# The first four expert weights issued ahead of GpSimd's wait for the queries of pair 4, and later landings entered in PE's plan

## Chip, cores and metric

One core of a Trainium2 chip. The metric is the device time of one execution in microseconds; the kernel before was run 13 times, and its time is the median of these. Engines are named as in the profile: PE (TensorE, matmul; PEld its weight loads), ACT (ScalarE), DVE (VectorE), POOL (GpSimd), SP (SyncE, here only issuing transfers).

## The reference

Two stages. The first is attention with 8 batches, 12 heads, 448 tokens and a head size of 64, with soft-capped scores and no mask. The second takes its output as 448 tokens of width 768 and runs four attention experts of head size 64 with a causal mask; a gate picks two of the four for each token and weighs them.

```python
scores = scale * np.matmul(q, k.transpose(0, 1, 3, 2))
scores = cap * np.tanh(scores / cap)
scores = scores - np.max(scores, axis=-1, keepdims=True)
attn = np.exp(scores)
attn = attn / (np.sum(attn, axis=-1, keepdims=True) + 1e-09)
attn_out = np.matmul(attn, v)
x = attn_out.transpose(0, 2, 1, 3).reshape(B, S, H * D)

logits = x @ w_gate
topk = np.argpartition(-logits, K, axis=-1)[..., :K]
...
for e in range(E):
    q = x @ wq[e]
    k = x @ wk[e]
    v = x @ wv[e]
    scores = scale * (q @ k.transpose(0, 2, 1))
    ...
    ye = a @ v @ wo[e]
    for kk in range(K):
        mask = topk[:, :, kk] == e
        out += mask[..., None] * w[:, :, kk:kk + 1] * ye
```

All inputs are float32. The weights `wq`, `wk` and `wv` are (4, 768, 64), `wo` is (4, 64, 768).

## The kernel before

**Pairs and batches.** The heads are taken two at a time: 48 pairs, 6 to a batch. For a pair, POOL casts queries, keys and values from float32 to float16 (`a_cast`, `a_castv`, lines 385 to 404; DVE does the queries of pairs 0 and 1), PE transposes queries and keys (`a_tr`, L414 to L421), DVE copies them out of PSUM, PE makes the scores in four parts (`fill`, L476 for the part of the tail keys, L480 for the rest), ACT takes tanh of each part (`tanh`, L510) and then one exponential over the pair (`expo`, L516), PE multiplies with the values (L544, L550), DVE divides, and PE transposes the result (L585) into `xT`, the second stage's input. Two score buffers stand between PE and ACT.

**The second stage.** When the six pairs of a batch are in `xT`, its expert work becomes available: `batch(b)` puts it into PE's list. The projections of queries and keys run for two experts at a time, r = 0 for experts 0 and 1 and r = 1 for experts 2 and 3 (`b_qk`, L724); the projection of values takes all four experts and the gate in one matmul of 260 columns (`b_v`, L640, tile `wvg`), so it needs the value weights of all four; scores and exponentials follow (L762, L781), then values, the transposes and the output projection (L863). The work of batch b runs among the pairs of batch b + 1. The last batch is ordered by a separate search at the end (`last_batch`).

**The weights.** They come in through transfers issued by POOL, which convert to float16 on the way (line 1067). The list `loads` holds sixteen, in this order: q and k of expert 0, q and k of expert 1, v of experts 0 to 3, q and k of expert 2, q and k of expert 3, o of experts 0 to 3. Below they are called q0, k0, v0 and so on. The transfers of a pair's queries, keys and values are issued by SP (L308, L312), from pair 4 on for two pairs at a time; they land in float32 buffers that the casts empty.

**What sets the order.** The program is one walk over ACT's order, `prog`: tanh and exponential of pair after pair. A pair's entry `("S", p)` calls `slot(p)`, which issues what goes with it, in this order: SP's loads some pairs ahead, POOL's cast of pair p + 4, two weights on POOL, constants (slots 4 and 5), and it puts the transposes, the value products and, at every sixth pair, the batch's projections into PE's list. Every engine runs its instructions in the order in which they were issued, so the two weights of slot 0 stand behind the cast of pair 4 in POOL's order.

PE's order is made when the program is built. `Plan` keeps a reckoned time for each engine (`plan.act`, `plan.pe`, `plan.dve`) and, in `plan.done`, a reckoned time at which each thing is ready; `step` takes from PE's list what can start earliest and, among what can start within 0.3 of that, what is due first. Matmuls on dummy data (`keep_warm`, L898) fill places where nothing else can start. The reckoned landing of a weight decides only where PE's work on it is put in the order; on the chip, PE waits at that place until the weight has landed. A weight kind with several transfers, such as `("w", "v")`, takes the value entered last.

In the planner's figures a pair takes ACT 2.83 for the four tanh parts and 2.71 for the exponential (`dur`), the walk starts at 7.0, and so slot 1 is called near 9.8, slot 2 near 15.4, and so on by 5.55.

Of the kernel before, what the change touches and what calls it, by code (L numbers as in the profile page):

```python
# [239 lines left out]
def kernel(  # L240
# [13 lines left out]
    nc = tc.nc  # L254
# [39 lines left out]
    def load(p, n=2):  # L294

        b, j = divmod(p, HP)
        h0, h1 = 2 * j, 2 * (j + n)
        qf = stage.tile([QP, 2 * n, QC * Dh], f32, name=f"qf_{p}", tag="qf")
        kf = stage.tile([128, 2 * n, KC * Dh], f32, name=f"kf_{p}", tag="kf")
        vf = stage.tile([128, 2 * n, KC * Dh], f32, name=f"vf_{p}", tag="vf")  # L300
        ktf = stage.tile([128, n, Dh], f32, name=f"ktf_{p}", tag="ktf")
        vtf = stage.tile([128, n, Dh], f32, name=f"vtf_{p}", tag="vtf")
        for i in range(n):
            h = slice(2 * i, 2 * i + 2)
            staged[p + i] = (qf[:, h], kf[:, h], vf[:, h], ktf[:, i], vtf[:, i])

        def rows(dst, src, c):
            return lambda eng: eng.dma_start(dst, src.rearrange("h (p c) d -> p h (c d)", c=c))  # L308

        def tails(dst, src, i):  # L310
            t = src[b, h0:h1, KM:S].rearrange("(j two) p d -> two p j d", two=2)
            return lambda eng: eng.dma_start(dst[64 * i : 64 * (i + 1)], t[i])  # L312

        return [
            rows(qf, q[b, h0:h1], QC), rows(kf, k[b, h0:h1, 0:KM], KC), tails(ktf, k, 0),
            tails(ktf, k, 1), rows(vf, v[b, h0:h1, 0:KM], KC), tails(vtf, v, 0), tails(vtf, v, 1),
        ]
# [6 lines left out]
    def ahead(p, n, since, more=4):  # L324

        new = range(p + n + more * (p > since), p + n + more * (p >= since) + 1)
        return [i for i in new if i < NP]
# [48 lines left out]
    def a_cast(p):  # L376
        if p >= NP:
            return
        eng = nc.vector if p < 2 else nc.gpsimd
        assert p < 8 or ("tr", p - 8) in plan.done  # L380
        assert p < 12 or ("pv", p - 12, 1) in plan.done
        qf, kf, vf, ktf, vtf = staged.pop(p)
        q16 = hd.tile([QP, QC, 2, Dh], f16, name=f"q16_{p}", tag="q16", bufs=8)
        k16 = hd.tile([128, KC, 2, Dh], f16, name=f"k16_{p}", tag="k16", bufs=8)
        eng.tensor_copy(q16, qf.rearrange("p h (c d) -> p c h d", c=QC))  # L385
        nc.gpsimd.tensor_copy(  # L386
            k16, kf.rearrange("p h (c d) -> p c h d", c=KC)
        )
        for g in range(2):
            r = slice(64 * g, 64 * (g + 1))  # L390
            eng.tensor_copy(ktz[p % 8][r, r], ktf[r, :])
        cast[p] = (q16, k16)
        vcast[p] = (vf, vtf)
        if p > 1:
            a_castv(p)
# [506 lines left out]
    plan = Plan()  # L902
# [35 lines left out]
    def b_const(i):  # L938
        if i == 0:
            nc.gpsimd.memset(ltm, 0.0)  # L940
            nc.gpsimd.affine_select(
                out=ltm, in_=ltm, compare_op=ALU.is_ge, fill=-60000.0, base=0,
                pattern=[[1, 128]], channel_multiplier=-1,
            )
        else:
            nc.vector.memset(vtL, 0.0)
            nc.vector.memset(vtL[64:128, :, Dh : Dh + 1], 1.0)
        nc.vector.memset(vtB[i], 0.0)
        nc.vector.memset(vtB[i][0:64, 0:E:2, Dh : Dh + 1], 1.0)
        nc.vector.memset(vtB[i][64:128, 1:E:2, Dh : Dh + 1], 1.0)  # L950
        for t in pB[2 * i : 2 * i + 2]:
            nc.vector.memset(t[:, 0:64], 0.0)
# [8 lines left out]
    loads = []  # L961
# [81 lines left out]
    for p in range(len(UNITS), NP + HP + 4):  # L1043
        nom.setdefault(("S", p), t)

    def slot(p):

        plan.work[:] = [u for u in plan.work if u["key"][0] != "warm"]
        n = 9 if p < 3 else 6 if p < 7 else 3 if p < 13 else 0
        for i in range(n):  # L1050
            plan.done["from", p, i] = nom["S", p] + 7.0 + 5.6 * i / n
            plan.add(("warm", p, i), 0.22, 0.0, [("from", p, i)], 1.0e9, keep_warm)
        if p % 2 == 0:
            for i in ahead(p, LOAD, DEEP):
                if i % 2 == 0:
                    for f in load(i):
                        f(nc.sync)
        for i in ahead(p, CAST, DEEP + 2):
            a_cast(i)
            plan.done[("cast", i)] = max(  # L1060
                5.65 * i + 1.5 if i < 12 else 0.0,
                plan.act + 4.0 + 3.5 * (i - p - CAST) * (p == DEEP + 2),
            )
        for _ in range(2):
            if loads:
                w, dst, src = loads.pop(0)
                nc.gpsimd.dma_start(dst, src)
                plan.done["w", w] = plan.act + 26.0
        if p in (4, 5):
            b_const(p - 4)  # L1070
        for i in (1, 2) if p == 0 else ahead(p, TR, DEEP + 4, 4):
            plan.add(("tr", i), 0.43, 0.95, [("cast", i)], nom["S", i] - 3.0, a_tr, i)
        if 1 <= p < len(UNITS):
            u = UNITS[p - 1]
            es = [("E", u)]
            due = nom["S", p + 1] + 2.0
            if isinstance(u, tuple):
                i = "AB".index(u[1])
                u = u[0]
                plan.parts(("pv", u, i), 2, 0.47, 0.55, es, due, a_pv, u, i)  # L1080
                d = [("pv", u, i)]
                plan.add(("xt", u, "AB"[i]), 0.12, 0.27, d, due, a_xt_part, u, i)
            else:
                plan.parts(("pv", u, 0), 2, 0.47, 0.55, es, due, a_pv, u, 0)
                d = [("pv", u, 0)]
                plan.parts(("pv", u, 1), 2, 0.47, 0.55, d, due, a_pv, u, 1)
                plan.add(("xt", u), 0.22, 0.35, [("pv", u, 1)], due, a_xt, u)
        if p >= HP and p % HP == 0 and p < NP:
            batch(p // HP - 1)
        if p == NP - 1:  # L1090
            last_qk()
        if p == NP:
            last_vg()
# [6 lines left out]
    def last_qk():  # L1100
        for r in range(2):
            g = ("qk", "A", r)
            due = nom["X", B - 1, r, 0] - 2.0
            for j in range(NDC):
                d = [x_of(j, "A"), ("w", ("q", r)), ("w", ("k", r))] + [(*g, j - 1)] * (j > 0)
                plan.add(
                    (*g, j), 0.22, 0.66 * (j == NDC - 1), d, due, qk_mm, "A", r, j,
                    aux={0: "open", NDC - 1: "close"}.get(j), group=g,
                )
# [10 lines left out]
    def batch(b):  # L1120
        x = ("xt", HP * b + HP - 1)
        t0, t1 = nom["X", b, 0, 0], nom["X", b, 1, 0]
        for r, t in enumerate((t0, t1)):
            plan.parts(("q", b, r), 3, 1.13, 0.55, [x, ("w", ("q", r))], t - 4.0, b_qk, b, r, "q")
            plan.parts(("k", b, r), 3, 1.13, 0.55, [x, ("w", ("k", r))], t - 4.0, b_qk, b, r, "k")
        for n in range(4):
            d = [("v", b, n - 1)] if n else [x, ("w", "v")]
            plan.parts(("v", b, n), 2, 0.66, 0.6, d, t0 + 2.0 * n, b_v, b, n)
        plan.add(("g1", b), 0.0, 1.0, [("v", b, 3)], t1 + 1.0, b_gate, b, aux=None)
        plan.add(("g", b), 0.0, 0.8, [("g1", b), ("G", b)], t1 + 3.0, b_gate2, b, aux=None)  # L1130
        for e in range(E):
            due = t1 + 6.0 + 3.0 * e
            d = [("X", b, e // 2, 1), ("g", b)] + [("pvB", b, e - 1)] * (e % 2)
            plan.add(("pvB", b, e), 0.31, 0.7, d, due, b_pv, b, e)
            if e % 2:
                plan.add(("oT", b, e // 2), 0.22, 0.35, [("pvB", b, e)], due, b_ot, b, e // 2)
        for n in range(4):
            for f in range(2):
                i = 2 * n + f
                d = [("oT", b, 1), ("w", "o")] if i == 0 else [("wo", b, *divmod(i - 1, 2))]  # L1140
                due = t1 + 19.0 + 1.5 * i
                plan.add(("wo", b, n, f), 0.33, 0.5, d, due, b_wo, b, n, f)
# [522 lines left out]
```

## Time and profile before

| | |
|---|---|
| median of 13 runs | 326.75 us |
| lowest and highest of the 13 | 322.79 and 331.34 us |
| time of the profiled execution | 328.0 us |
| its span in the profile | 326.2 us |
| PE busy | 285.9 us (88%) |
| DVE busy | 217.8 us (67%) |
| POOL busy | 157.9 us (48%) |
| share of the chain that ended last: ACT, PE, DMA | 67%, 19%, 4% |
| DMA share in the windows 20 to 30, 30 to 40, 40 to 50 and 50 to 60 us | 1.15, 1.40, 1.61, 1.37 |

The span is what the profile covers of the execution; the execution's own time has a little more around it. An engine's order of time gives each instruction's start and length, its line and operation, and in brackets how long the engine had stood idle before it and what it then waited for. A window's row gives the busy time of each engine with its number of instructions, then the clock granted to PE as a share of full speed, the mean busy share of the 16 DMA engines, and GB/s. [...] Queue 1 is that of SP's transfers, queue 0 that of POOL's.

### The profile page before, as it was taken

The page shows a single profiled execution, that of the slowest core. Times are in us where ns is not written, and L with a number is a line of the kernel's source. Part 1 is how long each engine was busy: PE and PEld are TensorE (multiplying, and loading weights), DVE is VectorE, ACT ScalarE, POOL GpSimd, SP SyncE. Part 2 cuts the span into 40 slices and gives each one's busy share as a digit, 9 for nine tenths or more (in the row PEclk, how much of TensorE's full clock was granted, in tenths as well). Part 3 has the DMA queues.
Part 4 walks back from the last instruction along what each step waited for, and adds up shares of the span by engine and source line. Part 5 has one row for each costly group of instructions (what it writes and reads, how often), then busy time and mean ns, then how long its engine had stood idle before and what let it go on. Part 6 is the DMA issues. An engine that isn't in the chain of part 4 may idle for free.

```text
span 326.2 us, 9088 instructions
## 1 busy us (share of the span) xinstructions
PE 285.9 (88%) x3439; PEld 179.7 (55%) x3439; DVE 217.8 (67%) x760; ACT 306.8 (94%) x311; POOL 157.9 (48%) x480
## 2 busy tenths in 40 slices
PE   8888874998999979998889969997899888999993
PEld 3455442655556555655646645655655664557762
DVE  4444440667776787669867886668766976578673
ACT  3999993899999999999999999999999999999973
POOL 3739999482923569982932568062915100220200
PEclk9999996999999999999999999999799999999998
DMA  7689999997012999759073852677011102020045
GB/s 165 172 225 234 215 219 224 218 221 174 2 51 99 254 260 248 208 179 234 4 193 123 222 144 87 183 219 193 3 50 70 53 2 97 2 75 2 3 169 171
DMA packets 65404, 46.22 MB, mean 142 GB/s; under 512 B 26000, under 2 KB 61968, under 8 KB 65360
## 3 DMA queue, kind: packets, MB, share of 16 engines
q1 hardware_dynamic: 54064, 43.28, 50.9%
q0 software_dynamic: 10512, 1.58, 6.9%
q10 hardware_dynamic: 784, 0.77, 0.8%
q8 instruction: 27, 0.44, 0.6%
q14 instruction: 17, 0.14, 0.1%
HBM read 36.19 MB, written 11.01 MB: 145 GB/s over the span
## 4 chain that ended last, share of the span: by engine, by line
ACT 67%; PE 19%; issue 5%; DMA 4%; DVE 2%; POOL 1%; DVEq 0%; POOLq 0%
ACT y L510 32%; ACT p L516 26%; ACT pBs L781 7%; DMA wvg<-in_moe_wv_dram 4%; PE vps L640 2%; PE wops L863 2%; PE pv L550 2%; PE dummy L898 2%; PE pv L544 1%; PE s L480 1%; PE kps L724 1%; PE qkA L1166 1%; PE qps L724 1%; PE s L476 1%; PE qkB L1166 1%
## 5 line engine op out<-in xcount | busy, mean ns | idle before, releaser
L510 ACT ACTIVATE y<-s 128x896 f16<-128x896 f32 (+1 forms) x176 | 138.5, 933 | 6.9 <-PE s L476 6.0
L516 ACT ACTIVATE p<-y 128x3136 f16<-128x3136 f16 x44 | 128.7, 2925 | 0.1
L789 POOL TENSOR_SCALAR_AFFINE_SELECT pBs<-pBs 128x128 f16<-128x128 f16 (+1 forms) x112 | 28.3, 279 | 110.5 <-ACT pBs L781 109.4
L550 PE MATMUL pv<-v16s,p 128*128 128x65 f16 x1056 | 56.3, 194 | 0.0
L480 PE MATMUL s<-qt,kt 64*128 64x448 f16 x264 | 47.5, 363 | 9.4 <-ACT y L510 7.2
L550 PEld LDWEIGHTS <-p 128*128 128x128 f16 x1056 | 47.6, 98 | 3.7 <-issue 0.2
L544 PE MATMUL pv<-vtzs,p 128*128 128x130 f16 x176 | 39.6, 225 | 9.4 <-ACT p L516 7.6
L559 DVE RECIPROCAL rc<-pv 128x4 f32<-128x4 f32 x96 | 17.3, 180 | 43.0 <-PE pv L550 41.9
L563 DVE TENSOR_TENSOR xk<-pv,rc 128x256 f16<-128x256 f32 x96 | 40.8, 425 | 3.3
L370 DVE COPY ob<-wops 128x384 f32<-128x384 f32 (+1 forms) x54 | 29.9, 554 | 6.9 <-PE wops L863 6.6
L640 PE MATMUL vps<-wvg,xT 128*128 128x260 f16 (+1 forms) x192 | 30.6, 277 | 4.2 <-DMA wvg<-in_moe_wv_dram 4.2
L544 PEld LDWEIGHTS <-p 128*128 128x128 f16 x176 | 17.1, 97 | 28.9 <-ACT p L516 15.8
L480 PEld LDWEIGHTS <-kt 64*128 64x128 f16 x264 | 16.0, 93 | 29.8 <-issue 23.0
L385 POOL CAST q<-qf 112x512 f16<-112x512 f32 x46 | 28.2, 613 | 7.2 <-DMA qf<-in_q_dram 5.4
L781 ACT ACTIVATE pBs<-sB 128x960 f16<-128x960 f32 (+1 forms) x28 | 30.7, 1112 | 0.0
L863 PE MATMUL wops<-wo,oT 128*128 128x384 f16 x128 | 30.6, 327 | 0.0
L399 POOL CAST v16s<-vf 128x384 f16<-128x384 f32 x48 | 24.4, 508 | 6.0 <-DMA vf<-in_v_dram 3.2
L386 POOL CAST k<-kf 128x384 f16<-128x384 f32 x48 | 24.4, 508 | 3.4 <-DMA kf<-in_k_dram 3.4
L370 DVE COPY xT<-xtp 128x448 f16<-128x448 f16 (+2 forms) x50 | 18.6, 374 | 8.7 <-PE xtp L585 7.7
L404 POOL CAST vtzs<-vtf 64x64 f16<-64x64 f32 x96 | 22.8, 238 | 2.9
L898 PE MATMUL dummy<-warm 128*128 128x512 f16 x67 | 22.1, 418 | 1.3 <-DVE warm L330 1.3
L640 PEld LDWEIGHTS <-xT 128*128 128x128 f16 x192 | 16.4, 98 | 11.7 <-DMA wvg<-in_moe_wv_dram 4.7
(180 smaller groups left out, 536.4 us busy)
## 6 DMA issues: line engine op xcount, KB each, us to landing
qf<-in_q_dram SPq DMA_DIRECT2D x22, 448.0 KB, 5.7
out_dram<-ob SPq DMA_DIRECT2D x23, 384.0 KB, 2.3
kf<-in_k_dram SPq DMA_DIRECT2D x22, 384.0 KB, 6.3
vf<-in_v_dram SPq DMA_DIRECT2D x22, 384.0 KB, 5.6
out_dram<-ob SPq DMA_DIRECT2D x8, 192.0 KB, 2.8
ktf<-in_k_dram SPq DMA_DIRECT2D x44, 32.0 KB, 5.4
vtf<-in_v_dram SPq DMA_DIRECT2D x44, 32.0 KB, 4.8
kf<-in_k_dram SPq DMA_DIRECT2D x4, 192.0 KB, 3.3
```

Source lines behind the costliest of these rows:

```text
L370: (nc.scalar.copy if act else nc.vector.tensor_copy)(dst, src)
L480: nc.tensor.matmul(sc[:, g, 0:S], kt[r, 128 * i : 128 * (i + 1)], qt[r, :], start=True, stop=True,)
L510: nc.scalar.activation(dst, src, AF.Tanh, scale=isc / capf)
L516: nc.scalar.activation(pt[:, 0:n], y.pop(u)[:, 0:n], AF.Exp, scale=capf)
L544: nc.tensor.matmul(pv[:, n, :, :], prob(p, w, 0, 0), vtz[p % 12], start=(n == 0), stop=False, skip_group_check=True,)
L550: nc.tensor.matmul(pv[:, n, g, :], prob(p, w, j, g), v16[p % 12][:, g, j - 1, :], start=False, stop=(j == KC), skip_group_check=True,)
L563: nc.vector.tensor_tensor(xt[p][:, 2 * i : 2 * i + 2, :, :], pv[:, :, :, 0:Dh], rc.broadcast_to((128, 2, 2, Dh)), ALU.mult,)
L640: nc.tensor.matmul(ps, xT[b][:, j, w : w + 128], wvg[:, j, 0 : ps.shape[1]], start=(j == 0 and first), stop=(j == NDC - 1), skip_group_che ...
L781: nc.scalar.activation(pb[:, o0 : o0 + n], st[b].pop(("sc", r, g))[:, 0:n], AF.Exp, scale=isc)
L789: nc.gpsimd.affine_select(out=blk, in_=blk, compare_op=ALU.is_ge, fill=0.0, base=0, pattern=[[1, n]], channel_multiplier=-1,)
L863: nc.tensor.matmul(ps, st[b]["oT", r][:, w : w + 128], wo2[r][:, f * (D // 2) : (f + 1) * (D // 2)], start=(r == 0), stop=(r == 1),)
L898: nc.tensor.matmul(dummy, warm[:, 0:128], warm, start=True, stop=True)
```

## The change

In slot 0, four weights (q0, k0, q1, k1) are issued before the cast of pair 4, where two were issued after it; they are entered in the plan as landed at 30.0. In every later slot two weights are issued behind the cast, as before, so that each later pair of weights goes one slot earlier: v0 and v1 in slot 1, v2 and v3 in slot 2, q2 and k2 in slot 3, q3 and k3 in slot 4, the output weights in slots 5 and 6. Their reckoned landing was 26 behind ACT's reckoned time; it becomes the later of 20 behind it and 37.0 + 4.2 p for slot p.

```diff
+    def load_weights(n, done):
+        for _ in range(min(n, len(loads))):
+            w, dst, src = loads.pop(0)
+            nc.gpsimd.dma_start(dst, src)
+            plan.done["w", w] = done
+
     def slot(p):
...
+        if p == 0:
+            load_weights(4, 30.0)
         for i in ahead(p, CAST, DEEP + 2):
             a_cast(i)
...
-        for _ in range(2):
-            if loads:
-                w, dst, src = loads.pop(0)
-                nc.gpsimd.dma_start(dst, src)
-                plan.done["w", w] = plan.act + 26.0
+        if p:
+            load_weights(2, max(plan.act + 20.0, 37.0 + 4.2 * p))
         if p in (4, 5):
             b_const(p - 4)
```

## The prediction

> **What bounds the kernel now.** I read the page's busy shares first, then the waits of each engine, then the order of time around the one long wait, then the DMA queues. The shares:
>
> ```profile
> span 326.2 us, 9088 instructions
> ...
> PE 285.9 (88%) x3439; PEld 179.7 (55%) x3439; DVE 217.8 (67%) x760; ACT 306.8 (94%) x311; POOL 157.9 (48%) x480
> ```
>
> ScalarE (ACT) is busy for 306.8 of 326.2 us; PE follows with 285.9, of which 22.1 are dummies (L898). From 7.24 us, its first tanh, to the tail at 310 us it has one stretch of idleness. The order of time on ScalarE (start, length, work, idle before it) shows it:
>
> ```profile
> 44.13 2.87 ACT L516 ACTIVATE p<-y 128x3136 f16<-128x3136 f16 x1
> 46.84 2.59 ACT L510 ACTIVATE y<-s 128x896 f16<-128x896 f32 x3
> 54.44 0.54 ACT L510 ACTIVATE y<-s 128x448 f16<-128x448 f32 x1 [5.02 <-PE s L476]
> 54.88 2.81 ACT L516 ACTIVATE p<-y 128x3136 f16<-128x3136 f16 x1
> 57.59 1.72 ACT L510 ACTIVATE y<-s 128x896 f16<-128x896 f32 x2
> 60.23 0.92 ACT L510 ACTIVATE y<-s 128x896 f16<-128x896 f32 x1 [0.93 <-PE s L480]
> 61.31 0.54 ACT L510 ACTIVATE y<-s 128x448 f16<-128x448 f32 x1 [0.16 <-PE s L476]
> ```
>
> The reader is to see three gaps, 5.02 + 0.93 + 0.16 = 6.11 us; nothing else but 0.34 us at 235.8 idles ScalarE in the middle of the run. Its waits are for scores from PE, so PE's order of time over the same place:
>
> ```profile
> 48.41 0.54 PE L724 MATMUL qps<-xT,wq 128*128 128x448 f16 x2
> 53.20 0.83 PE L640 MATMUL vps<-wvg,xT 128*128 128x260 f16 x3 [4.25 <-DMA wvg<-in_moe_wv_dram]
> 53.82 0.58 PE L476 MATMUL s<-qt,kt 128*128 128x448 f16 x1
> ```
>
> PE had the first batch's queries begun, came to the projection on the value weights (L640) at 48.95 and stood 4.25 us for the last of them. The next scores (L476, pair 8) are behind it in PE's order, so ScalarE ran dry. The windows around it give PE's granted clock, the number before the DMA share:
>
> ```profile
> 48.90:53.20 4.30, 0.05 (x2) 0.01 (x1) 0.36 (x1) 0.52 (x1) 4.07 (x11) 0.72 1.52 238
> 53.20:57.20 4.00, 4.00 (x25) 1.97 (x26) 0.00 (x0) 2.76 (x2) 3.72 (x11) 0.50 1.38 208
> ```
>
> After the wait PE ran at 0.50, with no idle time: the 0.93 and 0.16 us that follow are this backlog. GpSimd's order of time says why the weights are late:
>
> ```profile
> 17.18 0.53 POOL L404 CAST vtzs<-vtf 64x64 f16<-64x64 f32 x2
> 21.55 0.61 POOL L385 CAST q<-qf 112x512 f16<-112x512 f32 x1 [3.84 <-DMA qf<-in_q_dram]
> 25.43 0.84 POOL L1067 DMA_DIRECT2D wq<-in_moe_wq_dram  x1
> 38.08 1.65 POOL L1067 DMA_DIRECT2D wvg<-in_moe_wv_dram  x2
> ```
>
> GpSimd waits 3.84 us for pair 4's queries, and only behind that cast come the weights. The issues looked up one at a time (start of issue plus time to landing) give the landings: q0 25.43 + 5.4 = 30.8; q1 29.66 + 10.2 = 39.9; v0 33.87 + 11.7 = 45.6; v2 38.08 + 12.8 = 50.9; v3 38.90 + 14.25 = 53.15 (the chain of waits gives this last one); q3 47.03 + 14.7 = 61.7; k3 47.88 + 17.9 = 65.8. Latency grows while spacing stays: the queue is backed up and delivers a weight every (53.15 - 30.8) / 7 = 3.2 us. What counts is when the queue starts, not when each weight is issued.
>
> **The change, part by part.** *The first four issues move ahead of the cast of pair 4.* Four at 0.83 us (row L1067) are 3.3 us, from 17.71, where the last cast before the wait ends, to 21.05. The cover is the 3.84 us wait, so they cost nothing on GpSimd, with 0.5 us to spare; without that cover the cast would be 3.3 us late. Queued behind are the casts of pairs 4, 5 and on, and PE's transposes wait for those. As two fewer issues lie between casts 4 and 5, cast 5 starts 1.65 us earlier, at about 25.5, and every later piece of GpSimd's order likewise as far as its data are there. SP's loads, which wait for these casts, aren't held by this.
>
> *The queue starts 7.7 us earlier* (25.43 to 17.75). At the same spacing v3 lands at 53.15 - 7.7 = 45.5. It must be issued in time: order is now four weights, casts 4 and 5, v0, v1, cast 6, v2, v3. Casts 5 and 6 take 2.55 us each, so v0 goes at about 28.0 and v3 at 33.0 if pair 6's data are there, at 34.0 if they are late as priced below; with the longest wvg time to landing, 14.25, that is 48.2. So 45.5 to 48.2, against 48.95 when PE gets there. I take 45.5, since the queue's spacing is the steadier row. **The wait of 4.25 goes whole**, with PE's cold stretch: -6.11 us on ScalarE.
>
> *What the earlier weights collide with.* Pair 4's loads are in flight: queries issued 15.78 (5.7 us), keys 16.38 (6.3 us, landing 22.7), and PE's transposes of pair 4 run at 23.49 to 24.1, right behind the key casts (the last ends at 23.69). The first weight's packets moved 2.5 us behind its issue (13 packets by 28.0, 771 in the next 2 us), so now from 20.2: the keys are exposed for 2.4 us. Rows: a value load issued at 24.06 was exposed for 1.8 us and took 5.7 us, no more than before (5.7 to 6.0); a query load issued at 26.04 was exposed 4.6 us and took 1.0 longer than its like (6.6 for 5.6); the keys at 26.74 1.5 longer. That is 0 to 0.23 us per us, for pair 4's keys 0 to 0.6 us. Slack behind the transposes is 0.67 us of PE idle and 0.15 at the next scores, 0.8 in all. Taken: 0. The worst row is a stretch where SP's queue moved 0.25 MB in 2 us (34 to 36) where it otherwise moved some 0.5: half speed, keys 2.4 late, 1.6 us lost on ScalarE. Nearest rows in time and kind are the first, so I keep 0 and hold 1.6 for the range.
>
> The Trainium skill speaks against this: its page "DMA: Bandwidth & Descriptors", section "Queues, rings and completion order", says that each DMA engine takes turns between the queues that have work, a packet at a time. By that rule two backed-up queues get equal turns, and pair 4's keys would go at half speed, 1.6 us lost and a time of 323.6 in place of 322.0. The row of 24.06 shows no such loss over 1.8 us, while the stretch of 34 to 36 looks like the rule.
>
> *Pair 6 and later.* Issued 21.05 to 24.06 by SP, landing 26.7 to 29.8 before; exposed from 20.2 on, at 0.23 per us they come up to 2.2 us late, 32.0 for the values. PE transposed pair 6 at 35.01, for which the key casts must be done. If loads took the worst measured 10.6 us, the keys of pair 6 (issued 21.65) would land at 32.3 and their two casts, about 1 us, end at 33.3: 1.7 us of cover are left. Pair 8 (transposed at 47.31, cast at 39.77 to 41.3) has more. Cost 0.
>
> *PE's order reckons otherwise.* Before, a weight was entered as landing 26 us behind ScalarE's planned time. With the planner's 5.55 us for a pair, slot 3 stands at 20.9 and the value weights at 46.9, 6 us too early against 53.15. Now slot 2's entry is 37 + 8.4 = 45.4, which is where I put v3. The second pair of experts (q2 to k3) goes from slot 5 (32 + 26 = 58.0; measured 65.8) to slot 4, 37 + 16.8 = 53.8. My landing for k3 is 17.75 + 5.4 + 11 x 3.2 = 58.3, for q3 55.1: the plan is 1.3 to 4.5 us too early there. Before, PE began that q at 66.68 and k at 71.25, which without the 6.1 us is 60.6 and 65.1. If the order stays, nothing waits. If it moves up to 53.8, q waits 1.3, and PE's dummies (at 60.71, 61.11 and 63.78, so three of them in this stretch) hide a part. Bounds 0 and 4.5; I take 0.6, nearer to the end where the order stays, since the value blocks come due first.
>
> *Everything else in the order* is planned by the same greedy walk from slightly other times; rows for its effect there are none. By the one ScalarE gap (0.34 us) between 62 and 310, and its tail gaps of 0.17 to 0.85, I bound it at -0.9 to +0.9 and take 0.
>
> **Sum.** Span 326.2 - 6.1 + 0.6 = 320.7. The profiled execution took 328.0, 1.8 more than its span: 322.5. That execution is 1.25 above the median of 326.75 and within 322.79 to 331.34. If the wait's length is what spreads the runs, the kernel after is at 322.5 whatever the run; if all runs spread alike, it is 321.3. I go between: **322.0**.
>
> **Rivals.** (1) *Part of the wait stays, or the second experts' weights take its place* (PE standing at L724 for k3). For it: the reckoned 53.8 against 58.3; against: the distance to 60.6. Half of what is won given back: 322.0 + 3 = 325.0, range 323.8 to 326.
>
> (2) *It doesn't do what it says*: the weights start earlier but the engines are full (DMA share over 1.0 from 20 to 70 us), so v3 lands at 53 anyway. For it: the weight spacing of 3.2 us is set by sharing; against: the packets are the same and the queue delivered its first weight in 5.4 us in the same full traffic. Time 326.75.
>
> (3) *Slower*: 4 x 768 small packets ahead of pair 4's and 6's loads starve the casts, PE stands at the transposes (L414) and ScalarE behind it. It decides once pair 4's keys come over 0.8 + 6.1 = 6.9 us late, at 29.6. For it: the transposes sit right on the casts. Against: the longest load in the busiest stretch took 10.6 for 6.3, 4.3 more, 3.5 us lost after the slack. With that delay back for pair 6 without its cover, another 4.3, and the planner's wait at k3 of 4.5 on top, 12.3 in all: 322.0 - 0.6 + 12.3 = 333.7; for the mechanism at the break-even of 6.9 it is 328, and I put the case at 331.
>
> **How the numbers follow.** Forecast 0.79, with its own range 320.2 to 323.7 (the 1.6 us above, 0.9 of order either way and half the spread below); rival 1 0.09, rival 2 0.06, rival 3 0.06. The range of 8 in 10 runs from 319.9 to 325.1, over most of rival 1. 0.5% of 326.75 is 1.6 us, about what a measurement of this kernel can tell from no change: faster means below 325.1, slower above 328.4. Faster 0.79 + 0.05 = 0.84; same 0.09 (the rest of rival 1, most of rival 2); slower 0.07.
>
> **What would show it.** In the profile after: first weight issue near 17.8 us; cast of pair 4's queries at 21.5 to 22.2; last wvg landing at 45 to 48; no wait at L640; PE's clock 1.0 from 48 to 57; ScalarE without a gap over 1 us up to 310; 94% busy to 96%. I am wrong if wvg still lands past 49, if ScalarE idles at 25 to 36, or if PE stands at L724 near 54 to 58.

## The result, and the profile after

| | before | after |
|---|---|---|
| median | 325.83 us (48 runs) | 321.29 us (11 runs) |
| lowest to highest | 322.42 to 331.34 us | 320.83 to 324.66 us |
| profiled execution, its span | 328.0 and 326.2 us | 321.09 and 319.3 us |
| ScalarE's gaps between 49 and 62 us in it | 6.11 us | none over 0.15 us |
| last value weight (v3) issued, landed | 38.90, 53.15 us | 34.50, 44.4 us |
| PE's first value matmul (L640) | 53.20, after 4.25 of waiting | 48.48, no wait |

The ratio of after to before is 0.9893, 95% interval 0.9862 to 0.9923: faster by 1.1%. It leaves out executions that took over 1.5% more than the fastest of their kernel; for the kernel before these are its longest, the profiled 328.0 among them, so the gain is smaller than the medians give (4.5 us, 1.4%). The prediction was 322.0 us, in a range of 319.9 to 325.1.

ScalarE's order of time after, at the place of the old gaps (start, length, instruction; an idle time would stand in brackets):

```profile
43.82 2.87 ACT L516 ACTIVATE p<-y 128x3136 f16<-128x3136 f16 x1
46.53 3.21 ACT L510 ACTIVATE y<-s 128x896 f16<-128x896 f32 x4
49.64 2.81 ACT L516 ACTIVATE p<-y 128x3136 f16<-128x3136 f16 x1
52.35 2.99 ACT L510 ACTIVATE y<-s 128x896 f16<-128x896 f32 x4
55.23 2.81 ACT L516 ACTIVATE p<-y 128x3136 f16<-128x3136 f16 x1
```

Four tanh parts and an exponential follow each other without a bracket, and an idle time of over 0.15 us would have one. From the first tanh at 6.92 us to the tail at 303 us there is none. PE's order of time after:

```profile
48.10 0.54 PE L724 MATMUL qps<-xT,wq 128*128 128x448 f16 x2
48.48 0.50 PE L640 MATMUL vps<-wvg,xT 128*128 128x260 f16 x3
48.81 0.35 PE L476 MATMUL s<-qt,kt 128*128 128x448 f16 x1
...
54.59 0.54 PE L724 MATMUL qps<-xT,wq 128*128 128x448 f16 x2
```

The same three pieces as before, in the same order, with no wait between them; the last line is the first use of the second experts' queries, which stood at 66.68 before. The windows after, granted clock before the DMA share:

```profile
48.90:53.20 4.30, 4.30 (x49) 2.42 (x47) 2.00 (x6) 4.21 (x5) 3.95 (x13) 1.00 1.37 220
53.20:57.20 4.00, 4.00 (x50) 2.51 (x46) 2.43 (x10) 4.00 (x5) 3.25 (x10) 1.00 1.19 192
```

The clock that fell to 0.72 and 0.50 stays at 1.00. GpSimd's order of time after:

```profile
17.83 0.84 POOL L1049 DMA_DIRECT2D wq<-in_moe_wq_dram  x1
...
20.28 0.85 POOL L1049 DMA_DIRECT2D wk<-in_moe_wk_dram  x1
21.17 0.61 POOL L385 CAST q<-qf 112x512 f16<-112x512 f32 x1
22.22 0.51 POOL L386 CAST k<-kf 128x384 f16<-128x384 f32 x1 [0.43 <-DMA kf<-in_k_dram]
22.67 0.53 POOL L391 CAST ktzs<-ktf 64x64 f16<-64x64 f32 x2
24.78 0.51 POOL L399 CAST v16s<-vf 128x384 f16<-128x384 f32 x1 [1.59 <-DMA vf<-in_v_dram]
...
33.67 1.65 POOL L1049 DMA_DIRECT2D wvg<-in_moe_wv_dram  x2
```

The four issues fill the old wait, and the query cast starts as they end. The values of pair 4 now come late (1.59 us), which nobody on the path waits for: ScalarE has no gap behind it.

### The profile page after: what moved, and what is told of

Same layout as the page of the kernel before. It is cut to its first block, busy times and chain, and to the rows that moved or that the text cites. A ratio compares the mean times of both kernels' runs of the same rounds, so it can differ in the third digit from the quotient of the medians.

```text
span 319.3 us, 9087 instructions
## 1 busy us (share of the span) xinstructions
PE 283.6 (89%) x3438; PEld 178.7 (56%) x3438; DVE 217.9 (68%) x760; ACT 306.5 (96%) x311; POOL 158.1 (50%) x480
## 4 chain that ended last, share of the span: by engine, by line
ACT 74%; PE 16%; issue 5%; DVE 1%; DMA 1%; POOL 1%; DVEq 0%; POOLq 0%
ACT y L510 35%; ACT p L516 30%; ACT pBs L781 7%; PE vps L640 2%; PE wops L863 2%; PE pv L550 2%; DMA qf<-in_q_dram 1%; PE s L480 1%; PE pv L544 1%; PE qkA L1171 1%; PE pvB L808 1%; PE qkB L1171 1%; PE sB L762 1%; PE kps L724 1%; PE xtp L608 1%
## 5 line engine op out<-in xcount | busy, mean ns | idle before, releaser
L640 PE MATMUL vps<-wvg,xT 128*128 128x260 f16 (+1 forms) x192 | 30.3, 275 | 0.0
L391 POOL CAST ktzs<-ktf 64x64 f16<-64x64 f32 x92 | 21.6, 234 | 2.7
L898 PE MATMUL dummy<-warm 128*128 128x512 f16 x66 | 21.0, 408 | 1.3 <-DVE warm L330 1.3
```

Of the source, the lines that this page charges most:

```text
L640: nc.tensor.matmul(ps, xT[b][:, j, w : w + 128], wvg[:, j, 0 : ps.shape[1]], start=(j == 0 and first), stop=(j == NDC - 1), skip_group_che ...
```

## The experiments

**The change has two halves: issues earlier, and other reckoned landings.** With the issues of the change and the old reckoning (26 behind ScalarE) the program built has the same instructions on all five engines as after, one by one. So the runs of the kernel after are also runs of that half alone: given the early issues, the new reckoning changes nothing. The other half alone:

```diff
 # issues where they were before, two a slot
-                plan.done["w", w] = plan.act + 26.0
+                plan.done["w", w] = max(plan.act + 20.0, 37.0 + 4.2 * p)
```

> The issues stay where they were before; only the reckoned landings are those of the change (slot p: the later of 20 behind ScalarE and 37 + 4.2 p). PE's order differs from before by one group of three value matmuls, which stands 58 matmuls later, near 53.9 us. Theory A (the gain is the value weights' landing against the place where PE asks for them, nothing else): v3 lands near 53.2 as before, PE stands under 0.5 us at L640, ScalarE idles under 1.5 us in all between 7 and 300 us, time 321.3 to 323.5. Rival B (the weights have to come earlier; the order alone does not help): PE stands at L640 or at L724 for 3 us or more, time 325 to 327.

Measured: 321.75 us median of ten (320.94 to 325.96), ratio 0.9903 (0.9852 to 0.9953). PE's order of time:

```profile
51.79 0.92 PE L724 MATMUL kps<-xT,wk 128*128 128x448 f16 x4
53.96 0.50 PE L640 MATMUL vps<-wvg,xT 128*128 128x260 f16 x3
```

and GpSimd's, with the issue as late as before:

```profile
37.65 1.64 POOL L1067 DMA_DIRECT2D wvg<-in_moe_wv_dram  x2
```

v3 was issued at 38.47 and landed 12.7 us later, at 51.2; PE, which has three value matmuls put behind other work, asks at 53.96. ScalarE has no gap there (0.31 us at 229, nothing else). That v3 happened to land 2 us earlier than on the page before does not explain it: in an execution of the kernel before v3 landed at 51.0, and ScalarE still lost 3.65 us (below). So the whole gain, within 0.5 us, is to be had without moving a transfer. Theory A holds; rival B falls. The cover is thin, though: in the profiled executions that issue v3 between 38.5 and 40.3 it landed from 51.0 to 53.4, the last half a microsecond before this order asks. Two of the ten executions took 324.87 and 325.96; neither was profiled, so what made them long stays open, as for the one of 324.66 among the eleven of the kernel after.

**The queue's start, or the weight's own issue?**

```diff
-            load_weights(4, 30.0)
+            load_weights(2, 30.0)
```

> Two weights ahead of the cast of pair 4 instead of four, so each later weight stays in the slot it had before; the reckoned landings are those of the change. PE's order is that of the kernel with the new plan alone. v3 is issued near 37.3, 1.6 us earlier than before. Theory A: PE asks for the value weights near 53.9, so nothing waits, ScalarE has no gap over 0.3 us, time 321.3 within 0.7. For the landings: if the queue's start sets them (the prediction's step, 3.2 us a weight from the first), v3 lands at 45.6; if each goes by its own issue plus the backlog in front of it, at 46.5 to 51. Rival B (four have to be ahead): PE stands at L640, time 323 or more.

Measured: 320.99 us median, ratio 0.9892 (0.98 to 0.9983, of four runs), no gap on ScalarE. GpSimd's order of time:

```profile
17.80 0.84 POOL L1049 DMA_DIRECT2D wq<-in_moe_wq_dram  x1 [0.21 <-issue]
...
29.63 0.82 POOL L1049 DMA_DIRECT2D wq<-in_moe_wq_dram  x1
...
38.03 1.64 POOL L1049 DMA_DIRECT2D wvg<-in_moe_wv_dram  x2
```

The queue started at 17.80 as after, yet v3 (issued 38.85) landed at 51.4 and not 45.6: the first two weights were in by 24.1, and the queue then stood empty until 29.63. That 51.4 is close to where v3 lands with no early issue at all (51.0 to 53.15 in the kernel before), so the queue's start bought little; v3's own issue and the weights still in front of it decide. The time is that of the kernel after all the same, since PE's order here is that of the plan alone and asks at 53.88.

**The price of lateness.**

```diff
-        for _ in range(2):
+        for _ in range(2 if p else 0):
...
-                plan.done["w", w] = plan.act + 26.0
+                plan.done["w", w] = plan.act + 20.45
```

> No weights in slot 0, each pair of weights one slot later than before; the reckoned landings lowered by 5.55, so that PE's order is the same as before, instruction for instruction. v3 is issued 4.2 us later, near 43.1. Theory A: it lands near 57.4, PE stands 8.5 us at L640, ScalarE's gaps add up to 10.3 us, time 4.2 over before (330, 329 to 332). Rival E (the landing is set by how full the DMA engines are, not by the issue): v3 lands at 53 to 55, time within 1.5 of before.

Measured: 329.1 us median, ratio 1.0137 (1.0036 to 1.0237). ScalarE's order of time shows its three gaps again:

```profile
57.04 0.54 ACT L510 ACTIVATE y<-s 128x448 f16<-128x448 f32 x1 [7.51 <-PE s L476]
63.21 0.92 ACT L510 ACTIVATE y<-s 128x896 f16<-128x896 f32 x1 [1.30 <-PE s L480]
64.29 0.54 ACT L510 ACTIVATE y<-s 128x448 f16<-128x448 f32 x1 [0.16 <-PE s L476]
```

They add up to 8.97 us. v3 was issued 3.05 later than before (41.95; I had said 4.2, but with two issues gone from slot 0 GpSimd runs ahead by part of it) and landed 2.6 later, at 55.75. The gaps grew by 2.86, the profiled time by 2.54, all against the profile before. That is near one to one for this pair of executions; v3's landing alone moves by 2 us between executions of the kernel before (below). The medians show a loss of 3.7 us (329.1 against 325.36 beside it), so rival E falls.

**Beyond the cover.** GpSimd's wait was 3.84 us, and four issues take 3.3. With six and with eight, in the same line of the code:

```diff
-            load_weights(4, 30.0)
+            load_weights(6, 30.0)
```

> Six weights ahead of the cast of pair 4. Six issues take 5.0 us from 17.8, so the casts of pair 4 begin near 22.8, 1.6 us later than after. If the slack behind pair 4's transposes is the 0.8 us of the prediction, ScalarE idles 0.8 us near 27 us and the time is 322.1; if it is the 2.2 us that eight weights ahead left (3.1 late, 0.88 lost), ScalarE has no gap and the time is that of the kernel after, 321.3 within 0.5.

```diff
-            load_weights(4, 30.0)
+            load_weights(8, 30.0)
```

> Eight weights ahead of the cast of pair 4 instead of four; PE's order is the same as after, instruction for instruction. Eight issues take 6.6 us from 17.8, 3.3 us more than the wait that hid four, so the casts of pair 4 begin at 24.4 instead of 21.2. Theory A with the prediction's slack of 0.8 us behind pair 4's transposes: PE stands at L414 some 2.5 us, ScalarE idles 2.4 us near 27 us and nowhere else, time 323.7 (322.9 to 324.8). Rival C (the slack is larger, since the score buffers run ahead): under 0.8 us of idling, time 321.0 to 322.2. Rival D (eight weights also starve pair 6's loads at half speed): a second gap near 33 to 38 us, time 325 or more.

Measured: six, 321.5 us median and no gap over 0.15 us, against 321.43 for the kernel after beside it. Eight, 322.97 us median, ratio 0.9947 (0.9907 to 0.9988). PE's order of time with eight:

```profile
24.99 0.37 PE L414 MATMUL tps<-ident,q 112*128 112x112 f16 x4 [1.45 <-POOL q L385]
25.91 0.23 PE L419 MATMUL tps<-ident,ktzs 128*128 128x128 f16 x1 [0.55 <-POOL ktzs L391]
```

and ScalarE's:

```profile
27.13 1.35 ACT L510 ACTIVATE y<-s 128x896 f16<-128x896 f32 x2 [0.88 <-PE s L480]
```

The query cast began 3.15 us later than after (24.32), the key casts were 2.66 later, and ScalarE lost 0.88 in the profiled execution, in the place where rival 3 of the prediction put it. The slack is thus 1.8 us from the key casts, not 0.8. Six ahead agrees: there the key casts ended 1.9 us later than after (25.10 against 23.20), and ScalarE lost less than 0.15. The idle time is just over rival C's 0.8, while the median lies at the low end of theory A's range, so neither fits whole. Part of the 1.7 us between the medians of eight ahead and after is not seen in this profile, whose execution was among the shortest (322.22); that remainder stays open. Rival D's second gap at 33 to 38 us did not come.

**Why the runs of the kernel before spread.** The same kernel three times more:

> The kernel before once more, for the spread of its runs (322.4 to 331.3) against the narrow one of the kernel after (320.8 to 322.0 in all but one). Theory A: what spreads is when v3 lands, so the time of this execution less ScalarE's gaps at 49 to 62 us is 321 to 322 whatever the time itself. Rival F (all of the run is now faster, now slower): the gaps stay at 6.1 us while the time differs.

> As before_again_1: by theory A the time less ScalarE's gaps is 321 to 322; by rival F the gaps stay at 6.1 us.

> As before_again_1: by theory A the time less ScalarE's gaps is 321 to 322; by rival F the gaps stay at 6.1 us.

| execution | time | ScalarE's gaps, 24 to 65 us | time less gaps |
|---|---|---|---|
| before (the page) | 328.0 | 5.02 + 0.93 + 0.16 = 6.11 | 321.9 |
| before again 1 | 326.91 | 3.39 + 1.80 + 0.16 = 5.35 | 321.6 |
| before again 2 | 324.88 | 2.44 + 1.05 + 0.16 = 3.65 | 321.2 |
| before again 3 | 326.38 | 3.98 + 0.49 + 0.16 = 4.63 | 321.8 |
| one slot later | 330.54 | 7.51 + 1.30 + 0.16 = 8.97 | 321.6 |
| eight ahead | 322.22 | 0.88 | 321.3 |
| plan only | 321.48 | 0 | 321.5 |
| two ahead | 320.88 | 0 | 320.9 |
| after | 321.09 | 0 | 321.1 |

The shortest of the three in PE's order of time:

```profile
51.02 0.51 PE L640 MATMUL vps<-wvg,xT 128*128 128x260 f16 x3 [2.19 <-DMA wvg<-in_moe_wv_dram]
```

With the gaps taken off, all nine stand within 320.9 to 321.9. The three other profiled executions agree: six ahead 321.5, and, of those below, 321.1 with dummies and 321.2 for the kernel after once more. In the executions profiled the spread is thus in these gaps; rival F falls.

The gaps do not follow the landing of v3 alone. In "before again 1" v3 landed at 51.7 and in "before again 3" at 52.1, yet the earlier landing lost more (5.35 against 4.63). The difference lies behind the wait, in PE's clock: windows set to its steps give a granted clock of 0.50 for 6.8 us in the first (51.15 to 57.97) and for 3.4 us in the other (51.81 to 55.23). So v3's landing and the length of the half clock together set the loss.

**The clock's share.** In the kernel before, dummies where PE stands still:

```diff
+        if (b, n, i) == (0, 0, 0):
+            keep_warm(18)
         if i == 0:
             s["vps", n] = bank([128, E * Dh + E], f32, f"vps_{b}_{n}")
```

> The kernel before with 18 dummy matmuls (some 3.9 us at full clock) put into PE's order just ahead of the first value matmul, in the place where PE stands still; everything else in PE's order is as before. PE asks for the weights near 52.9 instead of 48.9. If the gaps of 0.93 and 0.16 us behind the wait come from PE's clock of 0.50, the clock stays at 1.0 through 48 to 57 and these two gaps shrink to under 0.3 us together, while the gap in front of pair 8's scores stays as v3's landing makes it (2.5 to 5.5 us; at least 3.9 less the slack even with early weights). If they come from the backlog alone, they stay near 1.1 us at clock 1.0.

Measured: 325.96 us in one execution. Its windows:

```profile
48.90:53.20 4.30, 3.83 (x18) 1.56 (x16) 0.26 (x1) 0.42 (x1) 4.07 (x11) 1.00 1.50 236
53.20:57.20 4.00, 3.77 (x35) 2.05 (x36) 1.35 (x4) 3.05 (x2) 3.77 (x10) 1.00 1.52 216
```

and its one gap on ScalarE in the whole stretch:

```profile
54.15 0.54 ACT L510 ACTIVATE y<-s 128x448 f16<-128x448 f32 x1 [4.84 <-PE s L476]
```

PE went on with the value projection as late as on the page before (53.20 there):

```profile
53.43 0.50 PE L640 MATMUL vps<-wvg,xT 128*128 128x260 f16 x3 [0.71 <-issue]
```

At clock 1.00 the two gaps behind the wait are gone, 1.1 us, though PE held up ScalarE for almost as long (4.84 against 5.02). The first gap has a share of the clock too: from PE's start on the values to ScalarE's next tanh it is 0.72 us here (53.43 to 54.15) and 1.24 before (53.20 to 54.44). So some 1.6 of the 6.11 us was PE's half clock, and 4.5 the wait itself. This is one execution.

**The kernel after once more**, beside six ahead:

> The kernel after once more, beside six weights ahead on the same chip. Theory A: no gap on ScalarE from 7 to 300 us, v3 lands at 44 to 47, time 320.8 to 322.0, while the kernel before beside it spreads over 3 us and more.

Measured: 321.43 us median of four (321.05 to 321.61); the kernel before beside it 324.76 to 327.38, a spread of 2.6 and not the 3 expected. v3 landed at 46.5 us (issued 36.2, 10.3 later), PE did not wait for it. There is one small thing new, in PE's waits:

```profile
PE qps L724 <- DMA wq<-in_moe_wq_dram: 0.4, 1, 0.4
```

It is the second experts' query weight, which the change's plan reckons early; ScalarE lost 0.23 us at 60.2, close behind it, where none was expected.

## Why the prediction was right, and where it was not

- *The wait of 4.25 goes whole, with PE's cold stretch: -6.11 us.* Right, and shown two ways (early issues, plan alone); the dummies show the clock's part in it. The profiled span fell by 6.9: these 6.11, the 0.34 at 235.8, a first tanh 0.32 earlier, and 0.1 that has no one place.
- *The size.* 322.5 from the profiled execution, 322.0 as told; the median is 321.29. Between 322.5 and the profiled 321.09 lie 1.4 us. The largest term that was off is the 0.6 for the second experts' weights: PE's order did move up (to 54.59), q3 landed at 53.1, and the wait was 0 in one profile and 0.4 in another. The 0.34 and the 0.32 above are the next two; the sum had nothing for them. k3 landed at 55.7 and was asked for at 63.0.
- *Going between the profiled run and the median.* The first reading, that the length of the wait spreads the runs, was the right one; the nine executions above show it. The kernel after was then to be put at the profiled sum, 322.5, whatever the median of before. The half step down to 322.0 has no ground in the runs; it came nearer only because the sum was too high by the terms above, and that was luck.
- *"What counts is when the queue starts, not when each weight is issued", v3 at 45.5.* v3 landed at 44.4 and 46.5, but the step is wrong, as two ahead shows (same start, v3 at 51.4). Four weights queued together landed 1.4 to 2.1 us apart (22.5, 23.9, 26.0, 27.6), not 3.2, and the queue ran empty before v0. The prediction's own landings weren't evenly spaced either: two weights took 9.1 us from q0 to q1 and 5.3 from v0 to v2. The landing came 8.75 us earlier because v3's issue is 4.4 us earlier and has fewer weights in front of it. That 45.5 came out near is luck: the other bound goes by v3's own issue, which was the better thought, and with its 14.25 us to landing it says 48.2, where the landing took 9.9.
- *Pair 4 costs 0.* Right on the path; the slack was larger (1.8) than the 0.8 that I counted from PE's idle time. A likely reason, not shown, is a tanh part that already lies ready in the second score buffer, about 0.8 us of ScalarE's work.
- *0 to 0.23 us late per us of exposure.* Too low early on. The DMA view from 20 to 22 us, first before, where only SP's queue moved anything, then after (q0 and q1 are the queues here; packets, MB, and the share of the 16 engines' time):

```profile
q1 hardware_dynamic: 919, 0.54, 106.1%
...
q0 software_dynamic: 1334, 0.17, 132.1%
q1 hardware_dynamic: 538, 0.25, 50.1%
```

  SP's queue moved less than half beside the weights: 0.25 MB for 0.54. The Trainium skill's page "DMA: Bandwidth & Descriptors", section "Queues, rings and completion order", says that each DMA engine takes turns between the queues that have work, a packet at a time. A loss of that kind fits it, but equal turns do not show: the profile counts 1334 packets of one queue to 538 of the other, and no run here shows what a turn is. Shares add up the packets' times, so packets that overlap take a share over 100%, also with one queue alone, as the 106.1% shows. Pair 6's queries and keys took 7.6 and 8.6 us where they took 5.6 and 6.4, and SP, which waited for those queries, issued the keys of pair 8 at 28.64 and not at 26.74. It cost nothing: pair 4's keys were nearly in, and ScalarE has no gap behind pairs 6 and 8.
- *PE's order as a cost.* This was the blind side: I weighed the new reckoning only as a risk (0 to 4.5 us). Alone it wins everything, since PE has other work to do while the weights land; and in the change as made the new figures do nothing at all.
- *Rivals.* Rival 1 shows at its smallest (0.4 us of PE). Rival 2 is excluded by v3's landing. Rival 3's place shows with eight weights (0.88 us seen, 1.7 between medians), but not its cause: the casts of pair 4's queries and keys follow the eight issues without waiting for data, so it is the issues on GpSimd that held them. Late loads show with six, where GpSimd waited 0.43 and 0.44 us for the tail keys of pair 4, and cost less than 0.15.

## What to carry to other kernels

A wait for a transfer has two ends: ask when the data come and also when the engine asks, and whether it has other work to do first; here either end alone was worth the whole gain. If the runs of a kernel spread by more than those of its neighbours, take the bottleneck engine's gaps off the time of each profiled execution: a constant remainder says that the gaps are the spread, and about what a version without them will take (here 320.9 to 321.9). Instructions moved into an existing wait are free up to that wait and the slack behind it, and not much further.

## What the runs showed of the hardware

- PE stood still for 2.19 us in "before again 2", up to 51.02 us. Its granted clock was still 1.00 for 1.5 us after that, then 0.50 from 52.52 to 55.93, with PE busy throughout. On the page before, where it stood for 4.25 us, the clock fell to 0.50 at 50.81, during the wait, and came back at 57.64. In the five profiled executions with a wait of over 2 us at this place the half clock lasted 3.4, 3.4, 6.8, 6.8 and 10.2 us, steps of 3.4, and not in the order of the waits: 2.19, 3.22, 2.62, 4.25 and 6.74 us.
- The length of an issue on SP moves between executions of one program. The two tail loads of the keys (L312) from about 17 us on took 1.32 us on the page before and 1.32, 3.00 and 3.01 in its three repeats, where GpSimd issues no weight before 25.4; with four weights issued beside them they took 1.98 and 2.65, with eight 2.94. What sets it stays open.
- A weight of 768 rows of 256 bytes took from 4.7 us (the first in the queue, after) to 17.9 us (in the backlog, before) to land, for the same 0.83 us of issue.
